# Sixty idle SyncE instructions behind an untaken branch, and identity matmuls in TensorE's early gaps: a two-headed attention and MoE kernel on one core

## The chip, the cores and the metric

The kernel runs on one core of a Trainium2 chip. The metric is the device time of one execution in microseconds (us). Each kernel is executed several times and the median is taken. Beside the times there is the profile of one execution: its span runs from the first to the last instruction of the program, and the device time of the same execution is a little longer than that span. Engines are written as in the profile: PE is TensorE (its matmuls; PEld are its weight loads), DVE is VectorE, ACT is ScalarE, POOL is GpSimd, SP is SyncE, which here issues all DMAs.

## What is computed

Attention over 4 batches, 8 heads, 768 positions and 64 dimensions per head, then a feed-forward layer. Three of the eight heads (`is_retrieval`) are causal over the whole sequence; the other five see 4 sink positions and a window of 64.

```python
scores = q @ k.T / sqrt(64)                       # per batch and head
mask   = causal if is_retrieval[h] else causal & (is_sink | in_window)
a      = softmax(where(mask, scores, -1e9))
x      = (a @ v) -> [4 * 768, 8 * 64]
out    = maximum(x @ w1, x @ w2) @ w_out          # 512 -> 1024 -> 512
```

## The kernel before

**Two programs behind a branch.** The kernel first reads `is_retrieval` and sorts the heads. If there are exactly three full heads (they are here) it takes the branch `tc.If(match >= 1)` (L830), a program that is made for this pattern: `run(..., exact=True)` at L837. The `Else` part (L838-839) holds a general program, `run(..., exact=False)`, which is not executed with these inputs but stands in every engine's instruction stream between the specialised program and the closing instructions. The profile books the closing instructions (waits for the outstanding DMAs, drains and a barrier of all engines) under L870. So at the end of the specialised program every engine jumps over the general program to its closing instructions.

**A plan, then an order written out.** `run` does not issue instructions itself. It collects operations (`P.op`, L63) with an estimated cost per engine, dependencies, buffers and a priority; `Plan.schedule` (L74) is a greedy list scheduler that gives each an engine, a start and an end on its own time axis, which I call the due times. The loop at L815 then emits all operations in the order of their due starts under `tc.manual_schedule()`, so that each engine's instructions stand in exactly that order. The framework adds the semaphore waits: an instruction waits until the earlier instructions that touch the same tile are done where they run on another engine. An engine never overtakes: an instruction that waits holds up all that stand behind it on its engine. Due times are not chip times; in the profile the due time 6.0 is at 10.2 us and the due time 28.4 at 35.3 us.

**The stages.** There are 16 units (4 batches, each with 4 pairs of heads). For each pair SP loads q, k and v; DVE or POOL casts them (`copy`, L296-300); PE transposes q and k through PSUM (`tr`, L689-693) or SP transposes by DMA; ACT or DVE copies the transposes to `qk` (L695-697); PE makes the scores (`score`, L570-587, with masks added by an identity matmul for the first batch at L586); ACT takes the exponentials (`ex`, L597-601); PE multiplies with v into a `po` tile (`av`, L619-625); DVE normalises out of that tile (`norm`, L635-643: a reciprocal L639 and two products L642). Beside this run the weights' casts, transposes of w2 (L449-456), a product of w2 and w_out (L461-467) and then the dense layers (L751-795).

**PSUM.** All eight banks are in use: two `sc` tiles of two banks, two `po` tiles and two `mm` tiles of one bank each. A `po` tile has 512 columns, of which attention uses 390 (2 heads x 3 blocks x 65). When the first two `norm`s are done (`units[0] == PO_TWO`, L648), one of the two `po` tiles is handed over to the `mm` pool for good (L649-652). From then on all `av` and all `norm` work on the single `po` tile that is left.

**The warm-up.** L413-419 puts one operation with 42 identity matmuls of 128 columns (`int(4.6 / 0.107)`) at the head of PE's order, into one of the two `mm` tiles, before any real work for PE has arrived.

Of the kernel before, what the change touches and what calls it, by code (L numbers as in the profile page):

```python
# [177 lines left out]
NORM = 0.80  # L178
PO_TWO = 2
DUO_FROM = 1  # L180
WARM = 4.6

SHIFT = {}
HOLD = {}
# [3 lines left out]
def kernel(  # L188
# [19 lines left out]
    nc = tc.nc  # L208
# [22 lines left out]
    def tl(name, shape, dt=BF16, n=None):  # L231
        if n is None:
            return sb.tile(shape, dt, name=name, tag=name)
        return [sb.tile(shape, dt, name=f"{name}{i}", tag=f"{name}{i}") for i in range(n)]

    def psum(name, n, banks=1):
        return [pp.tile([128, banks, 512], F32, name=f"{name}{i}", tag=f"{name}{i}") for i in range(n)]

    ident = tl("ident", [128, 128])
# [51 lines left out]
    po_t = psum("po", 2)  # L291
# [84 lines left out]
    def run(full, head, col, exact):  # L376
        P = Plan(*((SHIFT, HOLD) if exact else ({}, {})))
# [4 lines left out]
        sc_p, po_p, mm_p = map(Pool, map(list, (sc_t, po_t, mm_t) if PO_TWO or not exact else (sc_t, po_t[:1], po_t[1:] + mm_t)))  # L382
# [27 lines left out]
                            in1=causal, op0=ALU.mult, op1=ALU.add)  # L410
            c_m = P.op(f, {"DVE": 5.0}, [d_ir], prio=-20)

        if exact:  # L413
            bk = Buf(mm_p)

            def warm(e, bk=bk):
                for _ in range(int(WARM / 0.107)):
                    nc.tensor.matmul(bk.t[:, 0, 0:128], lhsT=ident, rhs=ident, start=True, stop=True)
            P.op(warm, {"PE": WARM}, (), [bk], prio=-100)
        d_w = {}  # L420
        for name in ("w2", "w1", "wo"):
            for c in range(4):
                if (name, c) in EARLY:
                    P.number += 1
                else:
                    d_w[name, c] = P.op(lambda e, name=name, c=c: load_weight(name, c), {"SP": 0.5},
                                        prio=LATER[name, c], size=0.524, rate=0.35)
# [18 lines left out]
        for fch in range(FC):  # L446
            bk = Buf(mm_p)
# [6 lines left out]
            o = P.op(tr, {"PE": 0.23}, w2_ops[2 * (fch // 4):2 * (fch // 4) + 2], [bk], prio=300 + fch)  # L454
            w2t_ops.append(P.op(lambda e, fch=fch, bk=bk: copy(e, w2t[:, fch, :], bk.t[:, 0].bitcast(BF16)[:, 0:d_model]),
                                {"DVE": 0.34, "ACT": 0.5}, [o] + wo_ops, [bk], prio=52 + fch))
        for c in range(KC):
            bk = Buf(mm_p)
            last = None
            for part in range(2):  # L460
# [4 lines left out]
                last = P.op(mm, {"PE": 0.865}, w2t_ops + wo_ops + [last], [bk], prio=320 + c)  # L465
# [1 line left out]
                               {"DVE": 0.63, "ACT": 0.49}, [last], [bk], prio=60 + c))  # L467

        xs, xt, xt_ops, norms = {}, {}, {}, {}
        last_exp, last_score, last, last_open, units = [None], [None], [None], [None], [0]  # L470

        def exp_op(emit, n, pointer, deps, bufs, prio):
            last_exp[0] = P.op(emit, {"ACT": n * 0.000833 + (0.14 if pointer else 0.06)},
# [47 lines left out]
        def attend(b, p, qk, vb, tk, ov, r):  # L521
# [110 lines left out]
            for u in range(2):  # L632
                rz = Buf(rz_p)

                def norm(e, u=u, rz=rz):  # L635
                    nh = 2 if exact else 1
                    p4 = po[u].t[:, 0, 0:nh * nn * (D + 1)].rearrange("p (h n e) -> p h n e", h=nh, e=D + 1)
                    rz_ = rz.t.rearrange("p (h n) -> p h n", h=nh)
                    V.reciprocal(out=rz_, in_=p4[:, :, :, D])  # L639
                    for i in range(nh):  # L640
                        h, n0 = (i, u * nn) if exact else (u, 0)
                        V.tensor_tensor(out=xs[b].t[:, n0:n0 + nn, bass.ds(col(s0 + h), D)], in0=p4[:, i, :, 0:D],  # L642
                                        in1=rz_[:, i].unsqueeze(2).to_broadcast([128, nn, D]), op=ALU.mult)
                done.append(P.op(norm, {"DVE": NORM}, [o for o in prev[u] if o], [po[u], rz, xs[b]], prio=r))
                for g in [u] if exact else range(NG):
                    norms[b][g].append(done[-1])
                units[0] += 1
                if exact and units[0] == PO_TWO:  # L648
                    spare = Buf(po_p)  # L649
                    spare.users = 1  # L650
                    P.op(lambda e: None, {"SP": 0.0}, [done[-1]], [spare], prio=-50).then = lambda: (
                        mm_p.free.append((spare.free, len(mm_p.tiles))), mm_p.tiles.append(spare.t))
            return done[-1]
# [4 lines left out]
        def pair(b, p):  # L658
# [53 lines left out]
            def fv(e):  # L712
                for h in range(2):
                    copy(e, vb.t[:, h, n0:, 0:D], raws[2].t[:, h, n0:])
            ov.append(P.op(fv, {"POOL": 0.58, "DVE": 0.48} if b == 0 else {"POOL": 0.95}, loads[2],
                           [raws[2], vb], prio=r + 0.05, shared=True))

            last[0] = attend(b, p, qk, vb, tk, ov, r)

        def x_turn(b):  # L720
# [89 lines left out]
                pool.free = []  # L810
        last[0].then = widen
        order = P.schedule()
        held = None
        with tc.manual_schedule():
            for o in order:  # L815
                for l in issued.values():
                    l.clear()
                o.emit(o.engine)
                if o.engine == "DVE" and o.shared:
                    held = issued["DVE"][-1]  # L820
                elif o.engine == "POOL" and held is not None:
                    tc.add_manual_dep(issued["POOL"][0], held.name, IN_TURN, reason="turns at the shared port")
                    held = None

    if not narrow:
        run([True] * H, lambda s: s, lambda s: s * D, False)
        return
    match = nc.values_load(perm[0:1, H:H + 1], min_val=0, max_val=1,
                           skip_runtime_bounds_check_because="a comparison")
    with tc.If(match >= 1) as branch:  # L830
        _, at = nc.values_load_multi_w_load_instructions(
            perm[0:1, 0:H], engines=(mybir.EngineType.SP, mybir.EngineType.Pool, mybir.EngineType.Activation), min_val=0, max_val=H - 1,
            skip_runtime_bounds_check_because="a permutation of the heads")
        _, xcol = nc.values_load_multi_w_load_instructions(
            pcol[0:1, 0:H], engines=(mybir.EngineType.DVE,), min_val=0, max_val=(H - 1) * D,
            skip_runtime_bounds_check_because="a permutation of the heads")
        run([s < FULL_SLOTS for s in range(H)], lambda s: at[s], lambda s: xcol[s], True)  # L837
    with branch.Else():  # L838
        run([True] * H, lambda s: s, lambda s: s * D, False)


# [33 lines left out]
```

## Time and profile before

| | us |
|---|---|
| median of 5 runs | 190.72 |
| lowest, highest | 189.03, 191.21 |
| profiled execution: device time | 190.23 |
| profiled execution: span | 188.5 |

| engine | busy us | share of the span |
|---|---|---|
| PE | 171.9 | 91% |
| ACT | 115.2 | 61% |
| DVE | 87.9 | 47% |
| POOL | 49.3 | 26% |

The profile cuts the span into 40 slices of 4.7 us and gives, for each, the busy tenths of every engine and the granted TensorE clock in tenths of full speed. The groups of instructions give the number of instructions of a line and the mean duration of one; for matmuls, which are pipelined, the distance from one start to the next is shorter than that duration. The chain that ended last names PE for 74% of the span and DMA for 7%. The last output DMA is issued at 182.31 us; the span ends at 188.5 us.

### The profile page before, as it was taken

Reading aid. Unit: us, or ns where it says so; the run is one execution under the profiler, and the core shown is the slowest. Engines: PE = TensorE matmul, PEld = TensorE weight load, DVE = VectorE, ACT = ScalarE, POOL = GpSimd, SP = SyncE. Lnnn points to the kernel's source line nnn. Section 1 sums busy time; section 2 is a strip of 40 time slices with the busy share of each in tenths; the row PEclk is TensorE's granted clock in tenths of the full one; section 3 lists DMA queues with packets and bytes.
Section 4 is the critical chain, followed back from the end, with each engine's and each line's share of the span. In section 5 each row is a group of like instructions: output and inputs, shape, how many; then the busy total and the mean of one; then the engine's idle time right before and its main releaser. Section 6 shows DMA issues by size and latency. Waiting matters only on the chain.

```text
span 188.5 us, 4604 instructions
## 1 busy us (share of the span) xinstructions
PE 171.9 (91%) x1663; PEld 100.3 (53%) x1663; DVE 87.9 (47%) x247; ACT 115.2 (61%) x191; POOL 49.3 (26%) x107
## 2 busy tenths in 40 slices
PE   1659999899999999999999999999999999999960
PEld 1635656656755655664565555456555545445440
DVE  5636785868788386435476364455741000000000
ACT  3237799878888678817893296469836427237120
POOL 2101050557895864532026325000000000000000
PEclk9955899999999999999999999999999999999995
DMA  5989999999999999999999999991019221021040
GB/s 120 288 272 345 282 267 379 288 298 292 319 311 249 212 232 228 227 254 182 258 242 194 266 202 253 210 264 47 3 57 224 59 110 57 0 111 59 0 174 9
DMA packets 79554, 36.96 MB, mean 196 GB/s; under 512 B 68642, under 2 KB 73506, under 8 KB 79522
## 3 DMA queue, kind: packets, MB, share of 16 engines
q1 hardware_dynamic: 79522, 36.58, 78.9%
q8 instruction: 15, 0.25, 0.5%
q14 instruction: 17, 0.14, 0.2%
HBM read 25.17 MB, written 6.29 MB: 167 GB/s over the span
## 4 chain that ended last, share of the span: by engine, by line
PE 74%; DMA 7%; POOL 4%; DVE 3%; issue 2%; SPq 1%; ACT 1%; DVEq 0%; POOLq 0%
PE mm L780 11%; PE mm L756 11%; PE sc L578 7%; PE po L623 7%; PE po L756 7%; PE po L780 7%; PE mm L787 5%; PE sc L780 4%; DMA raw<-in_moe_w_dram 3%; PE po L787 3%; DMA ld<-in_q_dram 3%; PE sc L756 2%; POOL wd_bf L443 2%; PE sc L787 2%; PE mm L692 2%
## 5 line engine op out<-in xcount | busy, mean ns | idle before, releaser
L599 ACT ACTIVATE at_all<-sc 128x1024 bf16<-128x1024 f32 (+2 forms) x72 | 59.6, 870 | 7.5 <-PE sc L578 3.5
L756 PEld LDWEIGHTS <-wd_bf 128*128 128x128 bf16 x256 | 23.2, 98 | 14.4 <-POOL wd_bf L443 0.3
L300 POOL CAST qb<-ld 128x384 bf16<-128x384 f32 x50 | 23.8, 507 | 17.0 <-DVE at_all L610 11.4
L756 PE MATMUL mm<-xt,wd_bf 128*128 128x384 bf16 x140 | 27.6, 326 | 0.1
L623 PE MATMUL po<-vb,at_all 128*128 128x65 bf16 x472 | 26.6, 197 | 0.7 <-DVE xs L642 0.4
L623 PEld LDWEIGHTS <-at_all 128*128 128x128 bf16 x472 | 22.0, 99 | 9.6 <-issue 1.7
L578 PE MATMUL sc<-qk 64*128 64x128 bf16 (+2 forms) x364 | 23.3, 242 | 1.4 <-ACT qk L298 0.9
L642 DVE TENSOR_TENSOR xs<-po,rz 128x192 f32 x64 | 22.9, 357 | 3.0 <-DVE rz L639 0.9
L780 PEld LDWEIGHTS <-raw 128*128 128x128 bf16 x152 | 14.1, 98 | 13.7
L578 PEld LDWEIGHTS <-qk 64*128 64x128 bf16 x364 | 12.6, 95 | 14.3 <-issue 9.6
L300 POOL CAST vb<-ld 128x384 bf16<-128x384 f32 (+1 forms) x28 | 12.8, 484 | 26.8 <-DMA ld<-in_v_dram 10.7
L639 DVE RECIPROCAL rz<-po 128x6 f32<-128x6 f32 x32 | 6.2, 193 | 26.8 <-PE po L623 26.8
L756 PE MATMUL po<-xt,wd_bf 128*128 128x384 bf16 x88 | 17.9, 326 | 0.0
L780 PE MATMUL mm<-wo_bf,raw 128*128 128x512 bf16 x64 | 16.1, 379 | 0.0
L610 DVE TENSOR_TENSOR at_all<-at_all,smk 128x1024 bf16<-128x1024 bf16 (+3 forms) x27 | 15.3, 584 | 0.0
L787 PEld LDWEIGHTS <-xt 128*128 128x128 bf16 x100 | 9.3, 97 | 9.3
L610 DVE TENSOR_TENSOR at_all<-at_all,tri 128x256 bf16<-128x256 bf16 (+1 forms) x36 | 9.8, 307 | 6.8 <-ACT at_all L599 6.7
L787 PE MATMUL mm<-wm_bf,xt 128*128 128x512 bf16 x48 | 12.3, 379 | 0.0
L298 ACT COPY ot<-mm 128x512 f32<-128x512 f32 x9 | 5.3, 585 | 11.1 <-PE mm L787 10.6
L764 ACT ACTIVATE raw<-mm 128x384 bf16<-128x384 f32 x20 | 9.8, 490 | 2.9 <-PE mm L756 2.6
L780 PE MATMUL po<-wo_bf,raw 128*128 128x512 bf16 (+1 forms) x48 | 11.3, 361 | 0.0
L298 ACT COPY qk<-mm 128x768 bf16<-128x768 bf16 x9 | 7.3, 807 | 5.9 <-PE mm L692 5.2
(91 smaller groups left out, 189.0 us busy)
## 6 DMA issues: line engine op xcount, KB each, us to landing
ld<-in_q_dram SPq DMA_DIRECT2D x32, 192.0 KB, 4.7
ld<-in_k_dram SPq DMA_DIRECT2D x32, 192.0 KB, 4.5
out_dram<-ot SPq DMA_DIRECT2D x23, 256.0 KB, 2.5
ld<-in_v_dram SPq DMA_DIRECT2D x24, 192.0 KB, 4.3
raw<-in_moe_w_dram SPq DMA_DIRECT2D x8, 512.0 KB, 6.7
raw<-in_moe_w_out_dram SPq DMA_DIRECT2D x4, 512.0 KB, 6.1
xt<-in_v_dram SPq DMA_DIRECT2D x3, 256.0 KB, 3.7
ld<-in_v_dram SPq DMA_DIRECT2D x8, 96.0 KB, 3.7
```

The source lines that it names most:

```text
L298: nc.scalar.copy(out=o, in_=i)
L300: issued[e].append((V if e == "DVE" else nc.gpsimd).tensor_copy(out=o, in_=i).ins)
L578: nc.tensor.matmul(sc.t[:, k, off:off + w], lhsT=qk.t[64 * h:64 * h + 64, 1, j * 128:(j + 1) * 128], rhs=qk.t[64 * h:64 * h + 64, 0, q0:q0 ...
L599: nc.scalar.activation(out=a.t[:, k:k + m, 0:n], in_=sc.t[:, k:k + m, 0:n], func=ACT.Exp, scale=scale, bias=0.0 if bias is None else bias[ ...
L610: issued["DVE"].append(V.tensor_mul(out=y, in0=y, in1=z).ins)
L623: nc.tensor.matmul(po[u].t[:, 0, o:o + D + 1], lhsT=a.t[:, k, off + t * 128:off + (t + 1) * 128], rhs=vb.t[:, h, j, :], **fresh(u))
L639: V.reciprocal(out=rz_, in_=p4[:, :, :, D])
L642: V.tensor_tensor(out=xs[b].t[:, n0:n0 + nn, bass.ds(col(s0 + h), D)], in0=p4[:, i, :, 0:D], in1=rz_[:, i].unsqueeze(2).to_broadcast([128, ...
L756: nc.tensor.matmul(bk.t[:, 0, 0:GT], lhsT=wd_bf[:, c, f * 128:(f + 1) * 128], rhs=xt[b].t[:, g * NB // NG:(g + 1) * NB // NG, c, :], start ...
L764: nc.scalar.activation(out=gt.t[:, f, :], in_=bk.t[:, 0, 0:GT], func=ACT.Relu)
L780: nc.tensor.matmul(bk.t[:, 0, 0:m1 - m0], lhsT=gt.t[:, f, t * 128:(t + 1) * 128], rhs=wo_bf[:, f, m0:m1], start=(f == 0), stop=False)
L787: nc.tensor.matmul(bk.t[:, 0, 0:m1 - m0], lhsT=xt[b].t[:, c0 // 128, c, :], rhs=wm_bf[:, c, m0:m1], start=False, stop=(c == KC - 1))
```

## The change

There are two parts.

1. After the general program, inside the `Else` branch, SP gets 60 `nop` instructions that cannot be fused (`PAD = 60`). The branch is not taken, so they are not executed; they move SP's closing instructions by 60 places.
2. The warm-up operation is taken out of the plan. Instead the loop that emits the plan looks at every PE operation: where the plan has PE idle for more than 0.2 us before it and the due end of the previous PE operation is under 45 (`WARM`), it first emits identity matmuls of 112 columns: 34 and one more per 0.059 of the gap beyond 3.7 for the first gap, one per 0.059 for the later ones. They write columns 400 to 511 of `spin`, the `po` tile that was not handed over, that is, of the one that `av` and `norm` keep using. Only those of the first gap carry `start=True`; the later ones add to what is there. Nothing reads those columns.

```diff
-WARM = 4.6
+WARM = 45.0
+PAD = 60
...
-        if exact:
-            bk = Buf(mm_p)
-
-            def warm(e, bk=bk):
-                for _ in range(int(WARM / 0.107)):
-                    nc.tensor.matmul(bk.t[:, 0, 0:128], lhsT=ident, rhs=ident, start=True, stop=True)
-            P.op(warm, {"PE": WARM}, (), [bk], prio=-100)
...
-        last_exp, last_score, last, last_open, units = [None], [None], [None], [None], [0]
+        last_exp, last_score, last, last_open, units, given = [None], [None], [None], [None], [0], []
...
                 if exact and units[0] == PO_TWO:
                     spare = Buf(po_p)
                     spare.users = 1
+                    given.append(spare)
...
         order = P.schedule()
-        held = None
+        held, idle = None, 0.0
+
+        spin = po_t[1 - given[0].slot if given else 0]
         with tc.manual_schedule():
             for o in order:
+                if exact and o.engine == "PE":
+
+                    gap = o.start - idle - 0.1
+                    if gap > 0.1 and idle < WARM:
+                        for _ in range(int(gap / 0.059) if idle else 34 + int((gap - 3.6) / 0.059)):
+                            nc.tensor.matmul(spin[:, 0, 400:512], lhsT=ident, rhs=ident[:, 0:112], start=not idle,
+                                             stop=True, skip_group_check=True)
+                    idle = o.end
...
     with branch.Else():
         run([True] * H, lambda s: s, lambda s: s * D, False)
+
+        with tc.manual_schedule():
+            for _ in range(PAD):
+                nc.sync.nop(nofuse=True)
```

## The prediction

> **What bounds the kernel now.** I read the slices first, then the windows, then the two ends of the program. The first rows to see: PE is busy almost throughout, but its clock is at half (tenths: 5) in the third and fourth slice.
>
> ```profile
> PE   1659999899999999999999999999999999999960
> PEclk9955899999999999999999999999999999999995
> ```
>
> Busy time by window (PE, PEld, DVE, ACT, POOL, then clock, DMA share, GB/s) dates this and shows the rest.
>
> ```profile
> 10.00:10.50 0.50, 0.32 (x5) 0.33 (x6) 0.12 (x1) 0.00 (x0) 0.00 (x0) 0.86 1.00 265
> 20.60:20.70 0.10, 0.10 (x6) 0.09 (x3) 0.00 (x0) 0.10 (x1) 0.00 (x0) 0.99 1.33 315
> 60.00:100.00 40.00, 40.00 (x427) 22.75 (x426) 23.39 (x65) 29.30 (x49) 17.48 (x39) 1.00 1.13 230
> 100.00:140.00 40.00, 40.00 (x387) 21.73 (x386) 20.98 (x60) 24.29 (x42) 8.12 (x18) 1.00 0.83 169
> ```
>
> A mean of 0.86 over 0.5 us means that the clock fell at about 10.36; it was back at 20.60. So 10.2 us ran at half speed. From 60 us PE has no idle time at all, and from 36 to 60 the windows leave it 0.5 us. Whatever moves PE at about 37 us therefore moves the end by the same, less at most 0.5.
>
> At the other end, SP's closing instructions and the instruction fetches (three answers for stretches of the end):
>
> ```profile
> L870 SPq EVENT_SEMAPHORE  x4: 17/28/28, 185.3 to 185.5; - x4
> q14 instruction: 1, 0.01, 1.5%
> L870 SPq EVENT_SEMAPHORE  x3: 28/28/28, 187.3 to 187.5; - x3
> ```
>
> The first row is from 185 to 186 us, the second from 185.5 to 187.3, the third from 187.0 to 187.5. SP runs four of its closing waits 0.07 us apart, stands still for 1.8 us while one instruction packet of 8 KB is fetched on q14, and goes on. The closing straddles two fetch lines.
>
> **Part 1, the idle instructions.** They are behind a branch that isn't taken and cost no execution. The cut is now behind the fourth closing instruction; 60 places on, the closing starts 56 places behind that cut, and its 13 instructions end at the 69th. Do 69 fit in a line? The page has 0.25 + 0.14 MB of instruction packets for 4604 instructions, 85 bytes each at most; 8 KB hold 96 or more. They fit. What goes is the stall: 187.3 - 185.5 = 1.8 us, less one normal step of 0.07. The line fetched for the jump itself remains (branch behind the last output DMA of 182.31 + 0.33, first closing wait 185.3), and nothing else is late behind the stall: ACT's drain ran at 184.4, PE's at 183.5. The bounds are 0 (the new place straddles as well) and -1.8; I take **-1.8**, since the row of the stall is there. [...]
>
> **Part 2, where the fills stand.** Without the warm-up operation the plan doesn't change: the first real PE operation is due at 6.03, after the warm-up's 4.6 + 0.26. So the due times of the kernel before (its planner's arithmetic, no chip time) give the gaps: 12 places, 73, 12, 18, 11, 5, 4, 7, 5, 11, 2, 1 and 3 matmuls, 152 in place of 42. Six transposes took 0.51 us with 0.219 for one, so (0.51 - 0.219) / 5 = 0.058 us from start to start; that is the price of one fill at full clock.
>
> **Places 1 to 4 (before 16 us).** The old 42 took 3.81 us from 4.20. The 73 take 6.6 us if all ran at that mean of 0.091, about 5.4 if those after 7 us run at 0.058: end between 9.6 and 10.8, before the first transposes (10.18) or 0.6 behind them. Cover: PE idles 2.18 us there, waiting for DVE's cast of q. The second and third take 0.7 and 1.0 in idle times of 0.62 and 0.89 us, which full speed widens by some 0.35 each; the fourth takes 0.6 while ACT works on the first exponential (1.02), whose tile the next scores need. I take nothing; without that cover it would be 0.6. What they bring is the clock: in the 3.4 us up to 10.4 PE was busy 1.22, now about 3.
>
> **What full clock is worth.** The q transposes at 16.57 wait for a cast that waits for its DMA; that stays. Behind it PE runs 4 us of work at half speed. But DVE sets what follows: its cast of k ends at 17.63, two copies of 0.96 give 19.55 instead of 20.19, and the first `norm` (reciprocal at 20.37, a register load, products until 21.93) ends at about 21.15, **0.8 earlier**.
>
> **What the fills wait for.** `norm` reads the tile that the fills write. A row of this kernel shows what PE does behind a `norm`: the `av` at 33.39 idled 0.41 for L642. A fill that is emitted behind a `norm` in the plan's order has to wait as well, and everything behind it on PE, even work that needs no `norm`. Bounds for each place: 0 (only bytes that overlap are ordered) and the full wait; I take the wait, by that row. [...]
>
> Three places have a `norm` of that tile due just before them (13.77 before 14.58, 20.17 before 20.27, 28.16 before 28.40). The rows (start, duration, engine, line, idle time before):
>
> ```profile
> 21.18 0.75 DVE L642 TENSOR_TENSOR xs<-po,rz 128x192 f32 x2 [0.62 <-DVE rz L639]
> 21.26 0.40 PE L578 MATMUL sc<-qk 64*128 64x384 bf16 x6
> ...
> 26.96 0.75 DVE L642 TENSOR_TENSOR xs<-po,rz 128x192 f32 x2
> 26.96 0.40 PE L578 MATMUL sc<-qk 64*128 64x128 bf16 x8 [0.27 <-DVE rz L639]
> ...
> 33.39 0.41 PE L623 MATMUL po<-vb,at_all 128*128 128x65 bf16 x8 [0.41 <-DVE xs L642]
> 35.26 0.40 PE L452 MATMUL mm<-ident,w_bf 128*128 128x128 bf16 x4 [0.30 <-DVE w_bf L300]
> ...
> 35.34 0.75 DVE L642 TENSOR_TENSOR xs<-po,rz 128x192 f32 x2
> ```
>
> In each pair PE's work started before `norm` was through; with a fill it can't.
>
> - Place 5 (5 matmuls): `norm` ends 21.15, + 5 x 0.058 = 21.45, + 0.1 to get going: the scores of the second pair at 21.55 instead of 21.26, **+0.3**. Left alone they would start at 19.65, when DVE's copies are done: the wait eats the gain of 1.6.
> - Place 7 (7): ACT's three exponentials (24.94, 2.14 long), fed by those scores, come 0.3 later; `norm` is fed by the first of them, has 0.3 to spare and still ends at 27.7. + 7 x 0.058 = 28.1, + 0.1: scores at 28.25 instead of 26.96, **+1.3** in all.
> - In between 0.7 is won back: `norm` of 32.37 stood behind DVE's cast of wo, for whose DMA DVE had idled 1.82 us. That one isn't later. The chain is 0.6 behind.
> - Place 9 (11) is the dearest: `norm` ends at 36.1 + 0.6 = 36.7, + 11 x 0.058 = 37.3, + 0.1: w2's transposes at 37.4 instead of 35.26, **+2.1** in all. They need only a cast (w_bf, done 35.2) and no `norm`.
> - The other places (4, 5, 2, 1 and 3 matmuls) stand in PE waits of 0.2 to 0.3 us or before an `av` that waits for `norm` itself: +0.2 together.
>
> From 37 us PE is full; of its 0.5 us idle I let it win back 0.3. Net of part 2: +2.1 + 0.2 - 0.3 = **+2.0** (between -0.8 and +2.8, where nothing is won back at 32 us).
>
> **Sum.** Profiled execution 190.23 (span 188.5 + 1.73 around it) - 1.8 + 2.0 = **190.4**, 0.3 under the median of 190.72 and well within its runs. A measurement of this kernel can tell about 1% from no change, so this is no change.
>
> **Rivals.**
>
> - *The fills cost nothing* (chance 0.28). They are held apart by columns, or `norm` is through earlier than I think, and PE finds each gap empty. For it: PE idles 2.7 us in small pieces between 20 and 37. Against: the rows above. Then part 2 is 0 to -0.8 (behind the wo cast at 31.76 most of the lead is lost to the DMA) and the time 187.6 to 188.4, middle 188.0.
> - *The clock falls again* (0.14), the slower side. PE now stands still behind three `norm`s, 1.5 us or more each. [...] If it falls in one of these stretches for 10.2 us as before, PE does about 9 us of work at half speed; some 4.5 us, of which the waits hide 1.5: +3.0, time 193.4. [...]
> - *The closing still straddles* (0.12): part 1 is nothing, 192.2 with my part 2.
> - My forecast (0.46): 189.3 to 191.2, the ends being 0.8 to 1.1 more or less won back around places 5 to 9.
>
> The range runs from 187.6 to 192.3: it takes in the forecast with both bounds of part 2, the first rival and the third, and leaves out the second and 0.04 or so at the ends. Chances: faster by over 1% (under 188.8) 0.30, the first rival and a little of the forecast; slower by over 1% (over 192.6) 0.18, the second and a part of the third; within 0.52.
>
> **What would show it.** Closing waits of SP all 0.07 us apart, about 3 us from its last output DMA to the first and 1.2 us from there to the end: part 1 right. PE's clock without a fall before the end: the fills do their work. PE idle for 1 to 2 us in front of identity matmuls, released by DVE's L642, at three places between 19 and 38 us: the waits; if those matmuls overlap L642, the first rival. PE's w2 transposes near 37.4 say whether the sum is right. It would be wrong if PE gets through 16 to 21 us much faster than I count, or if DMA, which is full until 140 us, hands the lost time back later.

## The result and the profile after

| | before | after |
|---|---|---|
| median, us | 189.88 (46 runs, 188.82 to 193.74) | 191.53 (25 runs, 190.68 to 196.12) |
| ratio of after to before, 95% interval | | 1.0088 (1.0068 to 1.0109) |
| profiled execution: device time, span, us | 190.23, 188.5 | 190.89, 189.0 |

The changed kernel is slower by 0.9%, 1.65 us. The forecast was 190.4, no change; 191.53 lies in its range, but its two parts did not do what I had counted on.

Slices of the changed kernel (busy tenths of PE, and the granted clock in tenths):

```profile
PE   1999879799999999999999999999999999999950
...
PEclk9999999999999999999999999999999999999996
```

The hole in the clock is gone: its record has full speed from 8.37 us to 185.86. The windows (PE, PEld, DVE, ACT, POOL, clock, DMA share, GB/s) say the same, and from 60 us on PE has no idle time, as before:

```profile
10.00:10.50 0.50, 0.17 (x3) 0.18 (x4) 0.34 (x2) 0.00 (x0) 0.00 (x0) 1.00 1.04 247
20.60:20.70 0.10, 0.10 (x3) 0.03 (x1) 0.10 (x2) 0.00 (x0) 0.00 (x0) 1.00 1.14 325
60.00:100.00 40.00, 40.00 (x429) 22.83 (x426) 23.33 (x64) 29.71 (x51) 17.68 (x39) 1.00 1.11 228
```

SP's closing instructions, in the stretches from 185 to 186 us and from 187.8 to 188.1 us (in the changed kernel they are booked under L879):

```profile
L879 SPq EVENT_SEMAPHORE  x4: 17/28/28, 185.6 to 185.8; - x4
L879 SPq EVENT_SEMAPHORE  x3: 28/28/28, 187.9 to 188.1; - x3
```

Four waits, a stall of 2.07 us, and the rest: part 1 has done nothing. The cut is still behind the fourth closing instruction. The reason is in the built programs: SP's general part has 263 instructions in both. The 60 `nop`s of the source never reach the chip.

The three places where fills wait for a `norm` are there as forecast (start, duration, engine, line, shapes, and idle time with what ended it):

```profile
19.00 0.75 DVE L636 TENSOR_TENSOR xs<-po,rz 128x192 f32 x2 [0.32 <-DVE rz L633]
19.80 0.41 PE L818 MATMUL po<-ident 128*128 128x112 bf16 x5 [0.84 <-DVE xs L636]
20.14 0.40 PE L572 MATMUL sc<-qk 64*128 64x384 bf16 x6
...
26.48 0.50 PE L818 MATMUL po<-ident 128*128 128x112 bf16 x7 [1.21 <-DVE xs L636]
26.92 0.40 PE L572 MATMUL sc<-qk 64*128 64x128 bf16 x8
...
34.63 0.75 DVE L636 TENSOR_TENSOR xs<-po,rz 128x192 f32 x2
35.44 0.70 PE L818 MATMUL po<-ident 128*128 128x112 bf16 x11 [1.07 <-DVE xs L636]
35.97 0.39 PE L446 MATMUL mm<-ident,w_bf 128*128 128x128 bf16 x4
```

L636 is `norm`, L818 are the fills, L572 the scores, L446 w2's transposes. PE stands still for 3.1 us in all behind `norm`, and the fills' own time of 0.06 us each comes on top. The scores start at 20.14 and 26.92 (before: 21.26 and 26.96), the transposes at 35.97 (before: 35.26). So the kernel is 1.1 us ahead at the first place, level at the second and 0.7 behind at the third.

The difference of the two profiled executions is smaller than that of the medians: PE's last matmul starts at 181.73 instead of 181.60, and from the last output DMA to the end of the execution it is 8.45 us instead of 7.92. Together 0.66. Single executions scatter by 1 us and more, in part by when loads land (the transposes at 16.57 before are at 15.75 after, at 17.16 in e9 below), so one pair of traces says where time goes, and only the medians say how much. Within that pair one place stands out: the last `av` before w2's transposes starts at 34.14 us in the changed kernel and at 34.73 before, and the transposes behind it at 35.97 and 35.26. A lead of 0.6 us has become a lag of 0.7 there.

### The profile page after: what moved, and what is told of

Its sections match the earlier page's. It is cut to its first block, busy times and chain, and to the rows that moved or that the text cites. A ratio compares the mean times of both kernels' runs of the same rounds, so it can differ in the third digit from the quotient of the medians.

```text
span 189.0 us, 4824 instructions
## 1 busy us (share of the span) xinstructions
PE 173.7 (92%) x1773; PEld 104.1 (55%) x1773; DVE 86.9 (46%) x247; ACT 114.8 (61%) x191; POOL 48.9 (26%) x107
## 4 chain that ended last, share of the span: by engine, by line
PE 80%; DVE 3%; DMA 3%; issue 0%; ACT 0%; DVEq 0%
PE mm L751 12%; PE mm L775 11%; PE sc L572 8%; PE po L617 8%; PE po L751 8%; PE po L775 7%; PE mm L782 5%; PE sc L775 4%; PE po L782 3%; PE mm L457 3%; DMA ld<-in_k_dram 3%; PE sc L751 2%; PE sc L782 2%; DVE xs L636 2%; PE sc L580 1%; PE mm L687 1%
## 5 line engine op out<-in xcount | busy, mean ns | idle before, releaser
L617 PE MATMUL po<-vb,at_all 128*128 128x65 bf16 x472 | 25.9, 194 | 0.0
L617 PEld LDWEIGHTS <-at_all 128*128 128x128 bf16 x472 | 21.2, 98 | 8.6 <-issue 0.6
L636 DVE TENSOR_TENSOR xs<-po,rz 128x192 f32 x64 | 22.9, 357 | 2.8 <-DVE rz L633 0.6
L572 PE MATMUL sc<-qk 64*128 64x128 bf16 (+2 forms) x364 | 22.2, 234 | 0.0
L572 PEld LDWEIGHTS <-qk 64*128 64x128 bf16 x364 | 12.3, 94 | 12.6 <-issue 9.0
L818 PE MATMUL po<-ident 128*128 128x112 bf16 x152 | 11.4, 238 | 7.4 <-DVE pcol L347 4.2
L818 PEld LDWEIGHTS <-ident 128*128 128x128 bf16 x152 | 10.1, 113 | 7.8 <-DVE pcol L347 4.2
L604 DVE TENSOR_TENSOR at_all<-at_all,tri 128x256 bf16<-128x256 bf16 (+1 forms) x36 | 8.4, 268 | 6.7 <-ACT at_all L593 6.7
```

What stands on the lines that cost most here:

```text
L572: nc.tensor.matmul(sc.t[:, k, off:off + w], lhsT=qk.t[64 * h:64 * h + 64, 1, j * 128:(j + 1) * 128], rhs=qk.t[64 * h:64 * h + 64, 0, q0:q0 ...
L604: issued["DVE"].append(V.tensor_mul(out=y, in0=y, in1=z).ins)
L617: nc.tensor.matmul(po[u].t[:, 0, o:o + D + 1], lhsT=a.t[:, k, off + t * 128:off + (t + 1) * 128], rhs=vb.t[:, h, j, :], **fresh(u))
L818: nc.tensor.matmul(spin[:, 0, 400:512], lhsT=ident, rhs=ident[:, 0:112], start=not idle, stop=True, skip_group_check=True)
```

## The experiments

The changed kernel and fifteen more. Each ratio is to the kernel before on the same chip, whose median there was 189.61 to 190.54 us, so kernels are best compared by their ratios. "Pad" means that SP gets 60 `drain`s where the change has `nop`s; `drain`s do reach the built program (323 instructions instead of 263 in e1). Places are the prediction's: 1 to 4 before 16 us, 5 to 8 up to 27, 9 before w2's transposes, 10 to 12 behind it.

| kernel | pad | warm-up | places | ratio to before, 95% interval |
|---|---|---|---|---|
| changed kernel | no | none | 1-12 | 1.0088 (1.0068 to 1.0109) |
| e1 | yes | 42 | none | 0.9888 (0.9855 to 0.9920) |
| e2 | yes | none | 1-12 | 0.9971 (0.9942 to 1.0000) |
| e3 | no | none | 1-4 | 1.0045 (1.0010 to 1.0079) |
| e4 | yes | none | 1-4 | 0.9919 (0.9886 to 0.9952) |
| e7 | yes | none | none | 0.9923 (0.9886 to 0.9961) |
| e14 | yes | none | 1 | 0.9956 (0.9911 to 1.0002) |
| e9 | no | none | 1-8 | 1.0055 (1.0024 to 1.0085) |
| e10 | no | 42 | 9 | 1.0057 (1.0023 to 1.0091) |
| e12 | no | 42 | 5-8 | 1.0055 (1.0021 to 1.0090) |
| e6 | no | none | 1-12, other tile | 1.0034 (0.9998 to 1.0071) |
| e11 | no | 42 | 9, other tile | 1.0032 (0.9997 to 1.0067) |
| e17 | no | 42 | 5-8, other tile | 1.0109 (1.0056 to 1.0162) |
| e16 | yes | none | 1-4 and 40 more | 0.9957 (0.9921 to 0.9993) |
| e13 | yes | 42 | none; one load more | 1.0024 (0.9987 to 1.0061) |
| e15 | no | 43 | none | 1.0026 (0.9990 to 1.0061) |

### Part 1 alone, and both parts with drains (e1, e2)

e1 is the kernel before with the pad; e2 is the changed kernel with its `nop`s replaced.

```diff
         run([True] * H, lambda s: s, lambda s: s * D, False)
+        with tc.manual_schedule():
+            for _ in range(PAD):
+                nc.sync.drain()
```

> The kernel before, with 60 drains of SyncE (a form of idle instruction that stays in the built program) behind the untaken general program, and nothing else. Theory: the closing straddles two fetch lines, and the 60 nops of the change never moved it, because none of them is in SyncE's built stream. Then this kernel's closing waits follow each other by 0.07 us without the stall of 1.8 to 2.1 us, the time from SyncE's last output DMA to the end falls from about 6.2 to 4.4 us, and the median is 1.8 us under that of before (about 188.1 for 189.9). Rival: the stall behind the fourth closing instruction belongs to the jump itself and not to its place; then it stays at 1.8 to 2.1 us and the time is that of before.

> The changed kernel with drains in place of its nops, so that both of its parts are there. Theory: 1.8 us under the changed kernel, 189.7 us, which is within 0.3 us of before (the fills' 1.6 us and the closing's 1.8 cancel, as in the forecast's sum). Rival (the stall belongs to the jump): 191.5 as the changed kernel.

e1: 188.39 us where before has 190.54 on the same chip, 2.1 us less. e2: 189.80. SP's closing in e1 (L875) and in the changed kernel (L879), each over the whole of it:

```profile
L875 SPq EVENT_SEMAPHORE  x10: 17/28/28, 184.4 to 185.7; - x10
```

```profile
L879 SPq EVENT_SEMAPHORE  x10: 17/28/28, 185.6 to 189.0; - x10
```

The same ten instructions take 1.3 us instead of 3.4; in e1 they stand 0.06 to 0.07 us apart up to the barrier of the engines. From the last output DMA to the end of the execution it is 187.50 - 181.42 = 6.08 us, where before had 190.23 - 182.31 = 7.92: the -1.84 that the prediction put on part 1. Its mechanism and its price are shown; what it lacked is an instruction that takes up a place. And e2 against e1 gives the price of part 2 by itself: 189.80 - 188.39 = 1.4 us, with intervals that do not overlap. Part 2 as a whole, the fills in and the old warm-up out, is what makes the changed kernel slow.

### Early full clock alone (e3, e4, e7, e14)

e3 is the changed kernel with the fills of places 1 to 4 alone, e4 the same with pad.

```diff
-WARM = 45.0
+WARM = 12.0
```

> The changed kernel with fills at the first four places alone (WARM = 12), 114 matmuls, none of them behind a norm of their tile. Theory: the late fills' waits for norm are what costs; without them the clock still stays at full speed from 7 us on and nothing waits: between 0.3 and 1.0 us under before, 188.9 to 189.6. Rival: the cost lies in the early fills themselves (fetching and running 73 matmuls in place of 42, or the place of the first transposes), then this kernel is 1 us or more over before, 190.9 or more.

> The first four places alone, and 60 drains behind the general program. Theory: the gains of the two add, 1.8 for the closing and 0.3 to 1.0 for the clock: 187.1 to 187.8 us, faster than both kernels. Rival: one of the two is nothing, then it is that of the other alone.

My theory by then, that the early clock would bring 0.3 to 1 us once nothing waits for `norm`, fell: e3 is 0.45% slower than before (191.51 us, where its rival had 190.9 or more), and e4 has 189.14 us instead of 187.1 to 187.8, 0.3% over e1, with intervals that overlap. The trace of e4 tells where the lead goes (DVE, POOL and PE around 28 us, e4 first, then the kernel before):

```profile
28.07 0.69 DVE L301 CAST w_bf<-raw 128x1024 bf16<-128x1024 f32 x1 [2.24 <-DMA raw<-in_moe_w_dram]
28.89 0.20 POOL L301 COPY qk<-qk 128x16 bf16<-128x16 bf16 x1 [3.22 <-DVE w_bf L301]
29.15 0.40 PE L572 MATMUL sc<-qk 64*128 64x128 bf16 x8 [2.28 <-POOL qk L301]
```

```profile
28.23 0.69 DVE L300 CAST w_bf<-raw 128x1024 bf16<-128x1024 f32 x1 [0.52 <-DMA raw<-in_moe_w_dram]
29.05 0.20 POOL L300 COPY qk<-qk 128x16 bf16<-128x16 bf16 x1 [1.81 <-PE po L623]
29.31 0.40 PE L578 MATMUL sc<-qk 64*128 64x128 bf16 x8 [0.21 <-POOL qk L300]
```

PE in e4 arrives 2.3 us early and then waits: the scores need a small copy on POOL, which keeps its turn behind DVE's cast of w2, which waits for w2's load. That load lands at about 28 us in either kernel. The scores start 0.16 us earlier than before, and that is all that full speed from 8 us on is worth there.

e7 goes the other way: pad, but neither warm-up nor fills.

```diff
-                    if gap > 0.1 and idle < WARM:
+                    if False:
```

> The kernel before with 60 drains on SP behind the general program and with neither warm-up nor fills: PE runs only the work itself. Theory A (PE's clock before 28 us is worth nothing, since the w2 load sets the work anew there): as with the drains alone, 188.0 to 189.0 us, 0.9 to 1.3% under the kernel before, although the clock stays at half to about 20 us or longer. Rival B (the early matmuls on identity cost by themselves): 187.0 to 187.9 us. Rival D (the warm-up is worth its place): 189.5 us or more.

188.46 us, within theory A's microseconds, but 0.77% under before, less than the 0.9 to 1.3% of that theory. By the intervals it can't be told from e1, although PE ran at half speed until about 18 us. The record of its clock begins at 18.14; before that the durations show the speed, six transposes each:

```profile
17.35 0.85 PE L687 MATMUL mm<-ident,qb 128*128 128x128 bf16 x6
...
21.77 0.51 PE L687 MATMUL mm<-ident,qb 128*128 128x128 bf16 x6 [0.20 <-DVE qb L301]
```

So neither the old warm-up nor the new one earns anything that these runs can measure: e1 (the old one), e4 (the new one) and e7 (none) have 0.9888, 0.9919 and 0.9923, and their intervals overlap. That e7 without a single fill equals e4 also says that the early fills need not be what puts e4 0.3% over e1. e14 (pad, the 73 matmuls of place 1 alone) was to tell which early fills cost.

```diff
-WARM = 45.0
+WARM = 0.5
```

> The kernel before with 60 drains on SP, the warm-up of 42 replaced by the 73 matmuls of place 1 and no other fills. Theory A (PE's early clock is worth nothing, and place 1 costs nothing): 0.988 to 0.990 of the kernel before, as with the drains alone. Rival B (the early fills cost 0.3 to 0.4%, and it is those of place 1): 0.991 to 0.993, as with places 1 to 4. Should it be 0.988 to 0.990, it is places 2 to 4 that cost.

0.9956, worse than both readings allowed for, with an interval as wide as 0.9%. Its profiled execution shows one way in which a lead can turn into a loss (the scores that wait for POOL, and a window of the clock):

```profile
29.93 0.61 PE L572 MATMUL sc<-qk 64*128 64x128 bf16 x8 [2.58 <-POOL qk L301]
```

```profile
29.28:36.10 6.82, 6.17 (x56) 3.67 (x57) 3.40 (x8) 4.29 (x6) 0.42 (x2) 0.50 1.04 359
```

PE arrived early, stood idle, and 2 us into that stretch the clock fell to half for 6.8 us, in which PE was 90% busy. e3's profiled execution, one of its longest (193.1 us), has the same after an idle stretch of 3.28 us (half clock from 32.32 to 35.73).

### The waits for the norm (e9, e10, e12)

e9 leaves out places 9 to 12, e10 adds place 9 alone to the kernel before, e12 places 5 to 8 alone. In e10 and e12 the old warm-up operation is in the plan as before. (Remarks in these cuts name the kernel.)

```diff
-WARM = 45.0
+WARM = 25.0                                  # e9
...
-                    if gap > 0.1 and idle < WARM:
+                    if gap > 0.1 and 27.0 < idle < 29.0:      # e10
+                    if gap > 0.1 and 12.0 < idle < 25.0:      # e12
```

> The changed kernel without its fills at places 9 to 12 (17 of 152 matmuls; the limit of 45 is 25). Theory A (the load of w2 sets the work anew at about 28 us, so that what places 5 and 7 cost is paid back there, and it is the wait of place 9's 11 matmuls, 1.07 us before and 11 x 0.05 us of their own, that makes the changed kernel slower): the w2 transposes begin at 34.4 to 35.3 us instead of 35.97, and the time is 189.9 to 190.7 us, within 0.3% of the kernel before. Rival B (the full clock and the early fills themselves cost, as the run with places 1 to 4 alone suggests): 191.0 to 191.8 us, as the changed kernel. Rival C (places 5 to 8 cost their 1.3 us after all): 191.0 us or more, with score 2.2 behind 30 us instead of 29.2.

> The kernel before, its warm-up of 42 matmuls and all, with the 11 matmuls of place 9 alone. Theory A: their wait for the cast of q comes at 34 to 36 us as in the changed kernel, the w2 transposes begin 0.7 to 1.6 us later than without them, and the time is 191.3 to 192.0 us, 0.5 to 0.9% above the kernel before. Rivals B and C: the matmuls of place 9 cost their own 0.6 us at most, 190.3 to 190.9 us, within 0.3%.

> The kernel before with its warm-up and with the 21 matmuls of places 5 to 8 alone (places 5 and 7 wait for the norm). Theory A (up to the landing of w2 at about 28 us the loads set the pace, and PE has time to spare): ratio 0.999 to 1.002, although PE waits at both places. Rival C (the forecast's step: +0.3 at place 5 and +1.0 at place 7, of which 0.7 comes back): ratio 1.003 to 1.007.

e10 answers for place 9: +0.57%, within theory A's 0.5 to 0.9%. Its 190.44 us lie in the rivals' range, since the kernel before had 189.61 there; it is the ratio that speaks for theory A, and the trace: the 11 matmuls wait 1.48 us for `norm`, and w2's transposes are at 35.89, where the kernel before has 35.26 and e1, the same program but for pad and fills, 34.65. e9 and e12 came out at +0.55%: e9 inside theory A's microseconds but outside its 0.3% of the kernel before, which was at 189.61 there (its profiled execution, 1.6 us over its median, had w2's cast only at 29.74 and can't settle it), and e12 where rival C had it. e12's trace shows why it was wrong to count places 5 and 7 as free:

```profile
21.33 0.41 PE L825 MATMUL po<-ident 128*128 128x112 bf16 x5 [0.84 <-DVE xs L643]
21.67 0.40 PE L579 MATMUL sc<-qk 64*128 64x384 bf16 x6
...
27.88 0.51 PE L825 MATMUL po<-ident 128*128 128x112 bf16 x7 [1.07 <-DVE xs L643]
28.31 0.40 PE L579 MATMUL sc<-qk 64*128 64x128 bf16 x8
```

With a granted mean of 0.970 (the changed kernel: 0.992) PE has no lead, and the same fills put the scores at 21.67 and 28.31. The prediction had 21.55 and 28.25 for the changed kernel. They are late by then for what the w2 load would have allowed: its cast starts at 28.28, as before (28.23), but the scores that wait for it start at 30.62 instead of 29.31. In the changed kernel the lead pays for both places; it is used up, not gained.

### The same fills in another tile (e6, e11, e17)

To take the wait away without making a race, the fills go into the PSUM tile that the PE work behind them takes anyway (tiles of the pools `sc` and `mm`): in e6 all of them, in e11 place 9, in e17 places 5 to 8.

```diff
+                        own = [x for x in o.bufs if x.pool in (sc_p, mm_p)]
+                        to = own[0].t[:, 0, 0:112] if own else spin[:, 0, 400:512]
...
-                            nc.tensor.matmul(spin[:, 0, 400:512], lhsT=ident, rhs=ident[:, 0:112], start=not idle,
+                            nc.tensor.matmul(to, lhsT=ident, rhs=ident[:, 0:112], start=bool(own) or not idle,
```

> The changed kernel with each fill written into the PSUM tile that the PE operation behind it takes (for the tiles of the pools sc and mm; the others as before), so that no fill waits for the casts of q out of the tile that the norm reads. The number of fills and their lengths are the same. Theory A: the waits of 0.84, 1.21 and 1.07 us at 19.80, 26.48 and 35.44 us go, the w2 transposes begin by 35.3 us, and the time is 189.9 to 190.9 us, within 0.3% of the kernel before. Rival B (early full clock and the fills' own time cost): 191.0 to 191.8 us, as the changed kernel.

> The kernel before with its warm-up and with the 11 matmuls of place 9 alone, but written into the tile of pool mm that the w2 transposes behind them take, in place of the tile that the norm reads. Theory A (place 9 costs by its wait for the casts of q out of the norm's tile, not by its own time): no wait before the fills, 189.5 to 190.0 us where the kernel before has 189.6, ratio 1.000 to 1.002. Rival (the 11 matmuls cost where they stand, whatever they wait for): ratio 1.004 to 1.007 as with place 9 in the norm's tile.

> The kernel before with its warm-up and the 21 matmuls of places 5 to 8, written into the tiles of pool sc or mm that the work behind them takes. Theory E (places 5 and 7 cost by their wait for the norm when PE has no lead): the waits of 0.98 and 1.22 us go, ratio 0.999 to 1.002. Rival (any matmuls there cost): ratio 1.004 to 1.007, as in the norm's tile.

At place 9 the trace is clear. e10 and e11 differ by the tile alone:

```profile
33.65 0.22 PE L624 MATMUL po<-vb,at_all 128*128 128x65 bf16 x2
35.35 0.70 PE L825 MATMUL po<-ident 128*128 128x112 bf16 x11 [1.48 <-DVE xs L643]
35.89 0.39 PE L453 MATMUL mm<-ident,w_bf 128*128 128x128 bf16 x4
```

```profile
33.91 0.23 PE L624 MATMUL po<-vb,at_all 128*128 128x65 bf16 x2
33.98 0.70 PE L827 MATMUL mm<-ident 128*128 128x112 bf16 x11
34.52 0.39 PE L453 MATMUL mm<-ident,w_bf 128*128 128x128 bf16 x4
```

The wait is gone, and w2's transposes start 0.6 us behind the `av` instead of 2.2. The times agree in direction, 1.0032 against 1.0057, but the intervals overlap, and 1.0032 lies between theory A (up to 1.002) and its rival (from 1.004). The same holds for e6, 1.0034 against the changed kernel's 1.0088: the intervals overlap by a hair. Places 5 to 8 in other tiles (e17, six runs) came out higher than in e12, 1.0109 against 1.0055, with overlapping intervals. There the tile is that of the scores, which ACT's exponential still reads:

```profile
28.33 0.50 PE L827 MATMUL sc<-ident 128*128 128x112 bf16 x7 [0.57 <-ACT at_all L600]
28.77 0.40 PE L579 MATMUL sc<-qk 64*128 64x128 bf16 x8
```

One wait is exchanged for another. The fills now come between the moment the tile gets free and the scores, and their whole length of 0.44 us (28.33 to 28.77) lies on the path from one exponential to the next. Theory E fell; neither of the two tiles tried at that place takes the fills for nothing.

### What sets the pace before 28 us (e13)

The kernel before with pad, and with the first quarter of moe_w2 (0.524 MB) loaded once more at about 9 us.

```diff
+TWICE_AT = 2
...
+        if name == "wo" and (name, c) not in EARLY and c == TWICE_AT:
+            load_weight("w2", 0)
```

> The kernel before with 60 drains on SP, and with the first quarter of moe_w2 (0.524 MB) loaded once more, behind the load of moe_w_out at about 9 us; the later load writes the same bytes again. Theory A (the DMA engines are full from 5 to 37 us, and the landing of w2 sets PE's pace): the w2 cast comes 1.5 to 1.9 us later (0.524 MB at 275 to 350 GB/s), and the time is 189.6 to 190.3 us, 1.2 to 1.9 us above the 188.4 of the drains alone. Rival (PE, DVE and ACT set the pace up to 37 us and loads have slack): 188.2 to 188.9 us.

190.64 us, a ratio of 1.0024 against e1's 0.9888: 1.4%, 2.6 us, more than theory A had and far from the rival. SP's closing has no stall in e13 either (6.43 us from the last output DMA to the end). In this pair of executions the cast of w2 is late by 2.1 us (e1, then e13):

```profile
27.84 0.69 DVE L301 CAST w_bf<-raw 128x1024 bf16<-128x1024 f32 x1 [0.27 <-DMA raw<-in_moe_w_dram]
```

```profile
29.95 0.69 DVE L302 CAST w_bf<-raw 128x1024 bf16<-128x1024 f32 x1 [0.58 <-DMA raw<-in_moe_w_dram]
```

The pair alone doesn't prove it, since without the extra bytes the same cast started at 29.7 to 30.3 us in the profiled executions of e3, e9, e16 and e17; the medians do. The 0.524 MB more moved the end by 2.6 us, where they take 1.6 to 1.9 us at the 278 to 329 GB/s of e13's windows between 5 and 30 us, and more speed on PE did not bring it forward (e4 0.9919, e1 0.9888). Until w2 had landed, the loads set the pace in these runs. Two windows of the kernel before had it (clock, DMA share and GB/s are the last three columns):

```profile
20.00:25.00 5.00, 4.92 (x83) 3.71 (x81) 4.10 (x14) 4.16 (x8) 0.71 (x3) 0.94 0.94 242
25.00:30.00 5.00, 4.37 (x54) 2.54 (x53) 4.10 (x9) 4.81 (x8) 2.12 (x7) 1.00 1.01 336
```

### Two controls (e15, e16)

e15 is the kernel before with one warm-up matmul more. e16 is e4 with 40 matmuls in front of the scores that wait for w2, into their own tile, so that PE doesn't stand idle there.

```diff
-                for _ in range(int(WARM / 0.107)):
+                for _ in range(43):                               # e15
...
-                    if gap > 0.1 and idle < WARM:
+                    if gap > 0.1 and (idle < WARM or 22.2 < idle < 22.4):     # e16: 40 at the second
```

> A control: the kernel before with 43 matmuls of warm-up in place of 42. If a part of what the other variants lost (0.3 to 0.6%) comes from any change at all of PE's program, the ratio is 1.003 to 1.006; if not, 0.998 to 1.002.

> 60 drains on SP, the fills of places 1 to 4, and 40 matmuls on ident before the scores that wait for w2's cast by way of POOL (due 22.72, started at 29.15 with places 1 to 4 alone), written into the tile that these scores take, so that PE does not stand idle for 2.3 us there. Theory D (with places 1 to 4 PE runs ahead, stands idle before 29 us, and in a part of the runs the clock then falls, as it did at 29.28 and 32.32 us in two profiled executions): no fall in the profiled execution, a granted mean of 0.99 or more in nearly all runs, ratio 0.985 to 0.990. Rival (the early fills cost by something else): ratio 0.991 to 0.995.

e15 came out at 1.0026, with an interval from 0.9990 to 1.0061. It neither clears nor convicts the mere change of PE's program, and it shows what a single row of the table can tell: 0.3% is not to be told from nothing. e16: 0.9957, no better than e4, and over the range of the rival too (0.991 to 0.995), so theory D isn't the cause, or its cure costs as much. In its profiled execution a load of k landed late (its cast started at 17.62 us, in e4 at 15.87), the clock fell from 19.01 to 22.43, PE had no lead, and the 40 matmuls (29.70 us, 2.13 long) simply stood in the way. Eight of its twelve runs had a granted mean of 0.996 or more, the other four 0.986 or less; the median of the eight is 188.9, which is still above e1.

## Why the prediction was right or wrong

- **Part 1, -1.8.** The step that failed is the first one, that 60 instructions of the source are 60 places in the stream. They are none: SP's general part has 263 instructions with and without them, and the stall was 2.07 us in the changed kernel where none was to be left. I asked whether 69 places fit into a line and never whether the `nop`s get there; the rival that part 1 does nothing was there with 192.2, but argued from a second cut; that its number is near is luck. Cut, stall and price were right, as e1 shows: -1.84 in the profiled execution, -2.1 in the medians.
- **Part 2, +2.0.** The waits are in the trace and the sum is near: +1.4 us by e2 against e1, +1.65 by the changed kernel, which has nothing else in it. With part 1 at nothing the prediction's own numbers give 192.2; measured 191.53. But that the size fits is in part luck: in the profiled execution w2's transposes are 0.7 us later and not 2.1, and the last matmul of PE 0.13.
- **Places 1 to 4 cost nothing, and the clock stays full.** The clock did: in the kernel before it was at half from 10.36 to 20.60 us, in the changed kernel it was full from 8.37 to 185.86. The 73 matmuls took 5.7 us (forecast 5.4 to 6.6). Whether these places are free isn't settled: e3 says +0.45%, e4 over e1 +0.3%, but e7, with no fills, is as far over e1, and the control has +0.26% for one matmul.
- **The first norm ends 0.8 earlier.** This is the mis-sized term: in the profiled execution it ended at 19.75 instead of 21.93, 2.2 earlier. Of this some 0.8 are loads of q and k that landed earlier in that execution, and 0.3 is a shorter step from the reciprocal to the products (0.32 idle instead of 0.62). The forecast had 21.15, 1.4 later, and all later steps are off by that much: scores 20.14 for 21.55, 26.92 for 28.25, transposes 35.97 for 37.4, each 1.3 to 1.4 us earlier than forecast. The waits themselves are at the places named, released by the line named. e12, without the lead, has the forecast's 21.55 and 28.25 to 0.12 us.
- **0.7 won back at the norm of 32.37.** The place was right in kind and too late: what resets the chain is the load of w2 at 28 us. It takes back leads, too, and I saw only that it forgives delays.
- **Place 9, the dearest.** Right: it is the only one of the three `norm` waits behind w2's landing, PE is the bound from there on, and e10 and e11 show its wait come and go.
- **0.3 won back after 37.** Between 45 and 65 us the lag of the changed kernel shrinks from 0.5 to 0.13 us; 0.4.
- **Rivals.** The first (fills held apart by columns) is out: PE waits (0.84, 1.21 and 1.07 us) although `norm` reads columns 0 to 389 and the fills write 400 to 511. (The 2.7 us that PE was to idle between 20 and 37 us are 1.5 by the windows, 15.49 busy of 17.) The wait here is the framework's, by tile (e11, with place 9's fills in another tile, has none), and no run shows what the chip would do without it. The second (the clock falls again) didn't happen in the changed kernel's trace, whose granted mean is 0.992, and only 3 of its 25 runs have a mean under 0.985. It did happen in other kernels with early fills, behind idle stretches for a load and not behind a `norm`: for w2 in e3 (3.28 us idle) and e14 (2.58), for w_out (ahead of q on DVE) in e9, for k in e16 (1.37). The fall that this rival took as its measure was 10.24 us long; those were 3.41 (e3, e9, e16) and 6.82 us (e14). The first entry of the kernel before's clock record, at full speed, is 3.41 us long, the second, at half, three times that. Here are the first and the thirds of the second:

```profile
6.95:10.36 3.41, 1.23 (x22) 1.06 (x20) 1.41 (x3) 0.57 (x3) 0.19 (x1) 1.00 0.89 267
10.36:13.77 3.41, 1.89 (x17) 0.96 (x15) 1.43 (x4) 1.60 (x2) 0.00 (x0) 0.50 0.88 268
13.77:17.19 3.42, 3.22 (x28) 1.93 (x27) 1.68 (x4) 2.74 (x3) 0.00 (x0) 0.50 1.06 327
17.19:20.60 3.41, 3.41 (x41) 2.41 (x40) 2.38 (x4) 1.98 (x3) 0.65 (x2) 0.50 1.06 338
```

PE's share is 36%, and the clock falls; then 55% and 94%, and it stays at half; then 100%, and it is back. In the changed kernel the emptiest piece of that length between 8.37 and 182 us had 69%, and the clock stayed full.

What stays open is how the 1.4 to 1.7 us divide. Places 5 to 8 cost 0.55% without the lead and 0.1% with it (e9 less e3), place 9 about 0.5%, and 0.3 to 0.45% stand against places 1 to 4 for which no trace gives a cause that holds. (In the pair of traces place 9 is the only one of the three waits behind which PE is later than before.) Each of these is at the edge of what twelve runs tell.

The best version is e1, the pad alone with an instruction that stays: 188.39 us, 0.9888 of the kernel before.

## What to carry to other kernels

Before you price an instruction that is there to take up room, see that it is in the built program. Before you speed up an engine in a stage, look for the transfer that everything in the stage will meet: here, with a DMA share of 0.99 to 1.01 between 25 and 30 us (e4, the kernel before) and an engine idle for it (`<-DMA raw<-in_moe_w_dram`), the lead became a longer wait (2.28 us in e4, 2.58 in e14), and during e14's wait the clock fell to half, for 6.82 us. Before you place a filler matmul, look who reads its tile: here DVE's `norm` read the `po` tile (waits of 0.84 to 1.48 us) and ACT's exponential the `sc` tile (0.57 us in e17), and PE's work behind the filler waited with it; in the `mm` tile of e11 there was no wait.

## What the runs showed of the hardware

- SP's way from its last output DMA to the first closing wait took 2.95 us in the kernel before (182.30 to 185.25) and 3.18 in the changed one (182.44 to 185.62). The stall behind the fourth closing wait was 1.87 us in the first (185.47 to 187.34) and 2.07 in the second (185.84 to 187.91), and in each of the two one instruction packet of 8 KB came in on q14. With the pad there was none: the ten waits took 1.3 us in e1 (184.4 to 185.7) and in e2 (186.6 to 187.9). 60 places were enough; how many it takes, no run measured.
- Half clock before 40 us lasted 3.41 us (e3, e9, e16), 6.82 (e14) and 10.24 (the kernel before). Ahead of the fall PE had been busy 1.23 of 3.41 us in the kernel before, 0.92 in e3, 1.48 in e14 and 1.53 of 3.42 in e16. In the last 3.41 us at half it was busy all the time in the kernel before, 3.40 us in e9 and 3.42 of 3.42 in e16. No run varied PE's share by itself, so these are cases and not a limit.
- Without any warm-up the clock was full 8.4 us after PE's first matmul (9.74 to 18.14 in e7; four scores took 0.61 us at 16.63 and 0.39 at 18.28). With the old warm-up of 42 matmuls it was full for good from 20.60 us in the kernel before, and in e13 the mean was still 0.71 between 20 and 25 us.
